# New load figures in a planner, and the order of loads and work that goes with them: retention and a gated layer on one core

## The chip, the cores and the metric

The kernel runs on 1 core of one Trainium2 chip. The metric is the device time of one execution in microseconds (us). The time before is 210.98 us, the median of 3 runs between 210.53 and 211.2 us. Below, PE is the engine that multiplies matrices (TensorE), DVE the vector engine, ACT the scalar engine, POOL the GpSimd engine, and SP the engine whose queue issues the loads.

## The reference

For each of 4 batches and 8 heads of 64 dimensions, a state of 64 x 64 decays at every one of 768 tokens and takes up the outer product of k and v; the token's output is q times that state. The 8 heads side by side are x (512 wide), and x goes through a gated layer.

```python
for t in range(S):
    state = gamma[None, :, None, None] * state + np.einsum('bhd,bhe->bhde', k[:, :, t], v[:, :, t])
    y[:, :, t] = scale * np.einsum('bhd,bhde->bhe', q[:, :, t], state)
...
for k in range(K):                      # K = 5 taps over the tokens
    gate_pre += conv_w[k][None, None, :] * xp[:, k:k + S, :]
gate = 1.0 / (1.0 + np.exp(-gate_pre))
val = x @ w_val
return (gate * val @ w_out).astype(np.float32)
```

## The kernel before, in words

The tokens are cut into 6 chunks of 128, so there are 24 pairs (chunk c, batch b), numbered g = 4c + b. One tile `att` of 1 MB holds for one g the transposed q and k, v by token, and k by token; four such tiles are in flight (`LB = 4`). A pair's retention is done in the chunked form: scores of q against k (into the PSUM tile `sy`), a mask on DVE (tile `u`), the product of the masked scores with v, the contribution of the state (`snap`, a copy of the PSUM tile `z_ps` made on ACT), and the update of the state in `z_ps`. Before a k or v is used for the state, POOL multiplies it by a decay table (`decay`, L355). The result y is multiplied on DVE by a table into x (`evac`, L519). Of x, ACT makes a rounded copy `xh` (L529), and POOL the rest `xl` (L534), so that a product in full precision is made from three products of rounded parts. The weights come as 64-bit numbers; each of the 8 weight tiles (`wst`, 0.5 MB) is converted by two operations on ACT (L559, L578), two on DVE (L563, L569), a sum on POOL (L582), then rounded on ACT (L592, `wvh` or `woh`), and POOL makes the rest (L596, `wvl` or `wol`). The five taps run on ACT (the first) and DVE (four, L610).

In the first chunk (g = 0 to 3) the state is empty. PE then has for each batch three blocks of 16 calls, all with small operands: the scores s (L379), the product y (L456, into the PSUM tile `ye`, of which there is one) and the two updates of the state z (L423). Later pairs are done in a visit v of 64 calls: the masked scores times v (L439), the state (L423), the state's contribution (L439), and the scores of the next pair (L366). The head h, scores (L366) and one half of a state update (L423) of g = 4, stands ahead of the first visit. The gated layer has 24 tiles V of 12 matmuls of 128 x 512 (`val`, L625) and 24 tiles O of 12 matmuls (`outp`, L659). V of chunk c and block m needs all four x of the chunk and the converted weight tile m: in order it takes `xh` with `wvh`, `xh` with `wvl`, `xl` with `wvh`. It writes one of two PSUM tiles `mm`, which comes free when DVE has multiplied the last one by the gate (`gated`, L640). The profile counts a call with 32-bit operands as two matmuls where they are small (a block of 16 calls is x32, a visit 128), and each matmul has a weight load of its own (PEld).

All of this is issued in an order that a planner in the program sets (`plan`, L79). Each step has an engine, a cost, what it reads and writes, and a due time. Due times come from two tables: LOADS (L704), the order of the first loads, and WORK (L707), a string in which p, s, y, z, h, v, V, O stand for the blocks above and w for a load and conversion of a weight tile. In LOADS, q is the q and k^T part of a batch of the first chunk (0.5 MB), v and k its v and k by token (0.25 MB each), a all but k (0.75 MB), t the small tables, w a weight tile. The planner then runs a model of the engines: whichever engine is free earliest takes, of the steps whose inputs are ready, the one with the lowest rank, and this gives the order in which the program lists the instructions. In the model a load lands `mb * PER_MB` after the load before it and not sooner than `FIRST_BYTE` after its issue (L246). Where the model sees PE wait ahead of the first V, it puts in filler matmuls on zeros (`filler`, L687, L689), whose results nothing uses. On the chip every engine then works off its own list in order, each instruction waiting for its inputs by semaphores.

SP issues all loads from one list, in order: a load waits until its buffer is free and until the load eight places ahead has landed. The tile of g = 4 goes into the buffer of g = 0 after its z, and so on.

Of the kernel before, what the change touches and what calls it, by code (L numbers as in the profile page):

```python
# [33 lines left out]
INTO, OUT_OF = 0.3, 0.134  # L34
COLD, WARM_AT = 1.85, 5.0
FIRST_PAGE, PAGE, FETCH, CROWDED = 94, 127.5, 3.0, 2.9
FIRST_BYTE, PER_MB = 4.1, 2.7
TABLES = (5.2, 9.3)

TIMES = {  # L40
# [222 lines left out]
def tile_retention_gated_mlp(  # L263
# [9 lines left out]
    nc = tc.nc  # L273
# [20 lines left out]
    small_sb = const.tile([P, small.shape[1]], F32, name="small_sb")  # L294
# [25 lines left out]
    def at(due, engine, cost, reads, writes, fn, *args):  # L320
        steps.append(Step(due, engine, cost, list(reads), list(writes), fn, args))
        return steps[-1]
# [371 lines left out]
    def first_sigmoid():  # L694
# [6 lines left out]


    CONV_LEAD, CHUNK = 7.0, 3.4
    LOADS = (("q", 0), ("t", 0), ("k", 0), ("v", 0), ("w", 0), ("a", 1), ("w", 1), ("a", 2), ("a", 3), ("k", 1), ("w", 2), ("k", 2), ("k", 3), ("w", 3))  # L704


    WORK = (  # L707
        "spysysszyyzzzVwwVwwhvVVOOvvOvOVvVvVVOvOvVVO"
        "vvVOvVvOVVOvOvVVOvvOVOvVOOvvvVVOVOOVVOVOOOO"
    )  # L710

    first_val = []
# [4 lines left out]
    def load_part_at(due, g, first, last):  # L717

        keys = [("att", g % LB, k) for k, part in (("qk", 0), ("vk", 2), ("kn", 3)) if first <= part < last]
        at(due, "DMA", 0.4, [], keys, load, g, slice(first, last)).mb = 0.25 * (last - first)  # L720
# [101 lines left out]
    def load_w_at(t, n):  # L822
        at(t, "DMA", 0.4, [], [wsts[n]], load_w, n).mb = 0.5
# [59 lines left out]
    at(0.2, "DVE", 0.25, [], [xbufs[0]] + [("x", 0, i) for i in range(B)], new_x, 0)  # L883
    for p, (kind, n) in enumerate(LOADS):
        t = 0.1 * p
        if kind == "t":
            at(t, "DMA", 0.4, [], ["small"], get, small_sb, small, nc.sync).mb = 0.2
        elif kind in "aqvk":
            load_part_at(t, n, *{"a": (0, 3), "q": (0, 2), "v": (2, 3), "k": (3, 4)}[kind])
        else:  # L890
            load_w_at(t, n)
    for x in range(2):
        for k, (engine, cost) in enumerate((("DVE", (0.42, 0.35)), ("ACT", (0.25, 0.2)))):
# [4 lines left out]
            )  # L898
    early = [n for kind, n in LOADS if kind == "w"]
    for n in ["cw"] + early:  # L900
        convert(5.5, n)

    t, whole = 6.0, {}
# [3 lines left out]
    for what in WORK:  # L907
# [7 lines left out]
        elif what == "s":  # L915
            t = max(t, 6.0 + CHUNK * i)
# [125 lines left out]
```

## Time and profile before

| | |
|---|---|
| runs | 210.98 us (210.53 to 211.2, 3 runs) |
| the profiled execution's own time | 210.8 us |
| its span | 209.0 us |
| PE busy | 199.7 us, 96% |
| DVE, ACT, POOL busy | 123.5, 110.2, 105.9 us |
| read from memory, written | 29.46 MB, 6.29 MB |

The span is the stretch from the first to the last recorded instruction; the execution's own time is 1.8 us longer. A line of the timeline gives the start in us, the duration in us, the engine, the line of the kernel, the operation, the tiles (written <- read), their shape and the count, and in brackets the idle time ahead of it and what ended it. Matmuls overlap: the start of the next line less the start of this one is what a line takes of PE's time.

### The profile page before, as it was taken

Reading aid. Unit: us, or ns where it says so; the run is one execution under the profiler, and the core shown is the slowest. Engines: PE = TensorE matmul, PEld = TensorE weight load, DVE = VectorE, ACT = ScalarE, POOL = GpSimd, SP = SyncE. Lnnn points to the kernel's source line nnn. Section 1 sums busy time; section 2 is a strip of 40 time slices with the busy share of each in tenths; the row PEclk is TensorE's granted clock in tenths of the full one; section 3 lists DMA queues with packets and bytes.
Section 4 is the critical chain, followed back from the end, with each engine's and each line's share of the span. In section 5 each row is a group of like instructions: output and inputs, shape, how many; then the busy total and the mean of one; then the engine's idle time right before and its main releaser. Section 6 shows DMA issues by size and latency. Waiting matters only on the chain.

```text
span 209.0 us, 7837 instructions
## 1 busy us (share of the span) xinstructions
PE 199.7 (96%) x3502; PEld 159.3 (76%) x3502; DVE 123.5 (59%) x189; ACT 110.2 (53%) x237; POOL 105.9 (51%) x93
## 2 busy tenths in 40 slices
PE   8967898999999999999999999999999999999994
PEld 3647676788888888788887888788787788878783
DVE  1586999952399814899129992227796259921100
ACT  3584687774667434685338654146364445413121
POOL 0189999999824582536627324526142353204200
PEclk9999999999999999999999999999999999999999
DMA  6999994557555508527275138348111100120122
GB/s 213 411 408 412 418 413 167 204 172 274 167 204 204 204 3 279 226 94 258 109 256 204 50 108 270 130 161 299 53 50 53 56 0 0 50 103 0 50 100 102
DMA packets 9253, 36.24 MB, mean 173 GB/s; under 512 B 1154, under 2 KB 1538, under 8 KB 6660
## 3 DMA queue, kind: packets, MB, share of 16 engines
q1 hardware_dynamic: 5472, 29.43, 37.7%
q10 hardware_dynamic: 3748, 6.32, 8.2%
q8 instruction: 27, 0.44, 0.9%
q14 instruction: 6, 0.05, 0.1%
HBM read 29.46 MB, written 6.29 MB: 171 GB/s over the span
## 4 chain that ended last, share of the span: by engine, by line
PE 89%; DMA 7%; issue 1%; DVE 1%; SPq 0%; ACT 0%; ACTq 0%
PE mm L659 33%; PE mm L625 33%; PE sy L439 11%; PE z_ps L423 5%; DMA att<-in_att_dram 5%; PE sy L366 5%; DMA cw_raw<-in_conv_w_dram 2%; PE sy L689 1%; PE sy L379 0%; DVE u L411 0%; PE ye L456 0%; DVE x L519 0%; SPq L342 0%; ACT gate L670 0%; SPq L545 0%
## 5 line engine op out<-in xcount | busy, mean ns | idle before, releaser
L610 DVE SCALAR_TENSOR_TENSOR acc<-x,cw_sb,acc 128x512 f32<-128x512 f32 x96 | 66.8, 750 | 2.7 <-ACT acc L608 2.1
L534 POOL TENSOR_TENSOR xl<-x,xh 128x512 fp32r<-128x512 f32 x24 | 30.9, 1288 | 44.0 <-ACT xh L529 44.0
L651 POOL TENSOR_TENSOR gvl<-gate,gvh 128x512 fp32r<-128x512 f32 x24 | 30.9, 1289 | 30.6 <-ACT gvh L647 30.6
L659 PE MATMUL mm<-woh,gvl 128*128 128x512 f32 (+1 forms) x100 | 38.7, 396 | 0.0
L659 PE MATMUL mm<-woh,gvh 128*128 128x512 f32 (+1 forms) x100 | 38.2, 390 | 0.0
L659 PE MATMUL mm<-wol,gvh 128*128 128x512 f32 (+1 forms) x100 | 37.9, 387 | 0.0
L625 PE MATMUL mm<-xl,wvh 128*128 128x512 f32 x96 | 34.4, 399 | 0.0
L625 PE MATMUL mm<-xh,wvh 128*128 128x512 f32 x96 | 32.0, 399 | 0.0
L355 POOL TENSOR_TENSOR att<-att,small_sb 128x512 f32<-128x512 f32 x24 | 25.1, 1049 | 12.4 <-DMA att<-in_att_dram 12.4
L640 DVE TENSOR_TENSOR gate<-mm,gate 128x512 f32<-128x512 f32 x24 | 16.5, 688 | 20.5 <-PE mm L625 18.1
L625 PE MATMUL mm<-xh,wvl 128*128 128x512 f32 x96 | 27.0, 397 | 0.0
L647 ACT CAST gvh<-gate 128x512 fp32r<-128x512 f32 x24 | 14.9, 619 | 22.1 <-DVE gate L640 22.0
L388 DVE TENSOR_TENSOR u<-sy,small_sb 128x512 f32<-128x512 f32 x20 | 13.7, 687 | 21.6 <-PE sy L366 21.6
L519 DVE TENSOR_TENSOR x<-sy,dec 128x512 f32<-128x512 f32 x20 | 13.7, 683 | 17.3 <-PE sy L366 12.5
L659 PEld LDWEIGHTS mm<-woh,gvl 128*128 128x128 f32 x100 | 18.7, 188 | 4.7 <-POOL gvl L651 0.5
L670 ACT COPY o_sb<-mm 128x512 f32<-128x512 f32 x23 | 13.5, 586 | 16.5 <-PE mm L659 16.1
L659 PEld LDWEIGHTS mm<-woh,gvh 128*128 128x128 f32 x100 | 18.7, 188 | 4.4 <-ACT o_sb L670 0.2
L617 ACT ACTIVATE gate<-acc 128x512 f32<-128x512 f32 x24 | 14.4, 600 | 14.1 <-DVE acc L610 7.8
L529 ACT CAST xh<-x 128x512 fp32r<-128x512 f32 x24 | 14.9, 619 | 13.0 <-DVE x L519 12.1
L659 PEld LDWEIGHTS mm<-wol,gvh 128*128 128x128 f32 x100 | 18.7, 188 | 3.8
L625 PEld LDWEIGHTS mm<-xl,wvh 128*128 128x128 f32 x96 | 18.0, 188 | 4.4
L625 PEld LDWEIGHTS mm<-xh,wvl 128*128 128x128 f32 x96 | 17.9, 188 | 4.3
(52 smaller groups left out, 248.2 us busy)
## 6 DMA issues: line engine op xcount, KB each, us to landing
att<-in_att_dram SPq DMA_DIRECT2D x20, 1024.0 KB, 5.3
out_dram<-o_sb ACTq DMA_DIRECT2D x23, 256.0 KB, 2.2
wst<-in_w_dram SPq DMA_DIRECT2D x8, 512.0 KB, 8.7
att<-in_att_dram SPq DMA_DIRECT2D x3, 768.0 KB, 7.2
att<-in_att_dram SPq DMA_DIRECT2D x5, 256.0 KB, 10.4
att<-in_att_dram SPq DMA_DIRECT2D x1, 512.0 KB, 3.6
out_dram<-gate ACTq DMA_DIRECT2D x2, 128.0 KB, 1.7
small_sb<-in_small_dram SPq DMA_DIRECT2D x1, 68.0 KB, 3.5
```

Source lines behind the costliest of these rows:

```text
L355: nc.gpsimd.tensor_tensor(v, v, vd_sb[:, c, :].unsqueeze(2).broadcast_to([P, 8, HALF]), op=ALU.mult)
L388: nc.vector.tensor_tensor(us[g], sy[:, :, 0:256].rearrange("p x (a t) -> p x a t", t=HALF), tri_sb.unsqueeze(1).unsqueeze(1).broadcast_to( ...
L439: nc.tensor.matmul(sy[cols, h, off:off + HALF], lhsT=lhsT, rhs=rhs, start=start, stop=True, skip_group_check=True,)
L529: nc.scalar.copy(xh[n][:, :, b], xs[n][:, :, b, HALO:])
L534: nc.gpsimd.tensor_tensor(xl[n][:, :, b], xs[n][:, :, b, HALO:], xh[n][:, :, b].bitcast(F32), op=ALU.subtract)
L610: nc.vector.scalar_tensor_tensor(acc, x[:, :, k:k + P], cw_sb[:, m, k:k + 1], acc, op0=ALU.mult, op1=ALU.add,)
L617: nc.scalar.activation(gate[n, m], accs.pop((n, m)), AF.Sigmoid)
L625: nc.tensor.matmul(vps[n, m], lhsT=w[:, m, ct * P:(ct + 1) * P], rhs=xx[n][:, ct].rearrange("p b t -> p (b t)"), start=(i == 0), stop=(i = ...
L640: nc.vector.tensor_tensor(gv, vps.pop((n, m)), gv, op=ALU.mult)
L647: nc.scalar.copy(gvs[n, m][0], gate[n, m])
L651: engine.tensor_tensor(gvl, gate.pop((n, m)), gvh.bitcast(F32), op=ALU.subtract)
L659: nc.tensor.matmul(ops[n, b, cs.start][:, 0:cs.stop - cs.start], lhsT=gg[:, b * P:(b + 1) * P], rhs=w[:, ct, cs], start=(i == 0), stop=(i ...
```

## The change

The planner's figures for loads are 3.0 us to the first byte and 2.65 us per MB instead of 4.1 and 2.7, the small tables count as 0.13 MB instead of 0.2, and the tables LOADS and WORK are others. No function, cost of an engine, tile or buffer is changed.

```diff
-FIRST_BYTE, PER_MB = 4.1, 2.7
+FIRST_BYTE, PER_MB = 3.0, 2.65
...
-    LOADS = (("q", 0), ("t", 0), ("k", 0), ("v", 0), ("w", 0), ("a", 1), ("w", 1), ("a", 2), ("a", 3), ("k", 1), ("w", 2), ("k", 2), ("k", 3), ("w", 3))
+    LOADS = (("q", 0), ("t", 0), ("v", 0), ("k", 0), ("a", 1), ("w", 0), ("w", 1), ("k", 1), ("k", 2), ("a", 2), ("k", 3), ("a", 3), ("w", 2), ("w", 3))
...
-        "spysysszyyzzzVwwVwwhvVVOOvvOvOVvVvVVOvOvVVO"
+        "spyszsyyzszyhVwzVwwVvwvVOvOvvOVOvvVVVvvOVvO"
...
-            at(t, "DMA", 0.4, [], ["small"], get, small_sb, small, nc.sync).mb = 0.2
+            at(t, "DMA", 0.4, [], ["small"], get, small_sb, small, nc.sync).mb = 0.13
```

The first place is PE's list around the first V. Before, with att_120, att_126 and att_129 the tiles of batches 1, 2 and 3 of the first chunk and att_206 that of g = 4, it reads:

```order
L423 MATMUL z_ps_94<-att_120 64x64 x16
L689 MATMUL sy_95<-const-float32-0.0 128x128 x4
L423 MATMUL z_ps_94<-att_126 64x64 x16
L625 MATMUL mm_428<-xh_217,wvh_89 128x512 x4
L423 MATMUL z_ps_94<-att_129 64x64 x16
L625 MATMUL mm_428<-xh_217,wvl_90 128x512 x4
L625 MATMUL mm_428<-xl_242,wvh_89 128x512 x4
L625 MATMUL mm_479<-xh_217,wvh_89 128x512 x4
L625 MATMUL mm_479<-xh_217,wvl_90 128x512 x4
L625 MATMUL mm_479<-xl_242,wvh_89 128x512 x4
L366 MATMUL sy_95<-att_206 64x64 x16
L423 MATMUL z_ps_94<-att_206 64x64 x8
```

Now, with att_128 and att_148 the tiles of batches 2 and 3 and att_218 that of g = 4, the same place reads:

```order
L423 MATMUL z_ps_94<-att_128 64x64 x16
L689 MATMUL sy_95<-const-float32-0.0 128x128 x4
L366 MATMUL sy_95<-att_218 64x64 x16
L423 MATMUL z_ps_94<-att_218 64x64 x8
L625 MATMUL mm_463<-xh_235,wvh_89 128x512 x4
L625 MATMUL mm_463<-xh_235,wvl_90 128x512 x4
L625 MATMUL mm_463<-xl_273,wvh_89 128x512 x3
L625 MATMUL mm_486<-xh_235,wvh_89 128x512
L625 MATMUL mm_463<-xl_273,wvh_89 128x512
L625 MATMUL mm_486<-xh_235,wvh_89 128x512
L423 MATMUL z_ps_94<-att_148 64x64 x16
```

The head of g = 4 has moved from behind the second V to ahead of the first; ahead of the first V stand the z of batches 0, 1 and 2 (the z of batch 1 earlier in the list), and that of batch 3 behind its fourteenth matmul, where before those of batches 2 and 3 stood around its first four.

The second place is POOL's list from its second instruction of the first chunk on, ending with the `xl` of batch 3. Before, it reads:

```order
L582 TENSOR_TENSOR cw_sb_87<-top_203,up_204 128x20
L534 TENSOR_TENSOR xl_242<-x_104,xh_217 128x4x128
L582 TENSOR_TENSOR top_209<-top_209,up_210 128x512
L582 TENSOR_TENSOR top_250<-top_250,up_251 128x512
L596 TENSOR_TENSOR wvl_90<-top_209,wvh_89 128x512
L534 TENSOR_TENSOR xl_242<-x_104,xh_217 128x4x128
L596 TENSOR_TENSOR wvl_90<-top_250,wvh_89 128x512
L355 TENSOR_TENSOR att_120<-att_120,small_sb_86 128x512
L534 TENSOR_TENSOR xl_242<-x_104,xh_217 128x4x128
L355 TENSOR_TENSOR att_126<-att_126,small_sb_86 128x512
L355 TENSOR_TENSOR att_129<-att_129,small_sb_86 128x512
L534 TENSOR_TENSOR xl_242<-x_104,xh_217 128x4x128
```

Now, with att_117 the tile of batch 1, it is one instruction longer; its first twelve rows are:

```order
L355 TENSOR_TENSOR att_117<-att_117,small_sb_86 128x512
L582 TENSOR_TENSOR cw_sb_87<-top_223,up_224 128x20
L582 TENSOR_TENSOR top_227<-top_227,up_228 128x512
L534 TENSOR_TENSOR xl_273<-x_104,xh_235 128x4x128
L596 TENSOR_TENSOR wvl_90<-top_227,wvh_89 128x512
L582 TENSOR_TENSOR top_268<-top_268,up_269 128x512
L534 TENSOR_TENSOR xl_273<-x_104,xh_235 128x4x128
L596 TENSOR_TENSOR wvl_90<-top_268,wvh_89 128x512
L355 TENSOR_TENSOR att_128<-att_128,small_sb_86 128x512
L534 TENSOR_TENSOR xl_273<-x_104,xh_235 128x4x128
L355 TENSOR_TENSOR att_218<-att_218,small_sb_86 128x512
L355 TENSOR_TENSOR att_148<-att_148,small_sb_86 128x512
```

The decay of batch 1 has moved to the front, and that of g = 4, which stood behind the first `xl` of batch 3, stands ahead of the decay of batch 3.

The third place is PE's list from the visit of g = 4 to that of g = 5. Now it reads:

```order
L439 MATMUL sy<-att,snap 64x64 x16
L366 MATMUL sy<-att 64x64 x16
L625 MATMUL mm<-xl,wvh 128x512 x4
L625 MATMUL mm<-xh,wvh 128x512 x4
L625 MATMUL mm<-xh,wvl 128x512
L439 MATMUL sy<-u,att 64x64 x16
```

Between the two visits stand 9 large matmuls; before there were 18. The numbers from visit to visit, from g = 4 on, are now 9, 11, 13, 11, 28, 7, 29, 7, 20, 24, 21, 7, 30, 38, 24, 12, 24, 57, 7, and before 18, 8, 21, 24, 12, 34, 8, 31, 12, 23, 12, 48, 12, 33, 7, 32, 30, 7, 7. After the last visit stand 177, before 173. In the list of loads on SP the first 14 follow LOADS; behind them stood g = 4, three weight tiles, g = 5 and 6, a weight tile, g = 7, and stand now g = 4, two weight tiles, g = 5, a weight tile, g = 6, a weight tile, g = 7.

More of the change, by code (lines that the diff above doesn't have):

```diff
@@ L703, in tile_retention_gated_mlp @@
     CONV_LEAD, CHUNK = 7.0, 3.4
-    LOADS = (("q", 0), ("t", 0), ("k", 0), ("v", 0), ("w", 0), ("a", 1), ("w", 1), ("a", 2), ("a", 3), ("k", 1), ("w", 2), ("k", 2), ("k", 3), ("w", 3))
+    LOADS = (("q", 0), ("t", 0), ("v", 0), ("k", 0), ("a", 1), ("w", 0), ("w", 1), ("k", 1), ("k", 2), ("a", 2), ("k", 3), ("a", 3), ("w", 2), ("w", 3))
     WORK = (
-        "spysysszyyzzzVwwVwwhvVVOOvvOvOVvVvVVOvOvVVO"
-        "vvVOvVvOVVOvOvVVOvvOVOvVOOvvvVVOVOOVVOVOOOO"
+        "spyszsyyzszyhVwzVwwVvwvVOvOvvOVOvvVVVvvOVvO"
+        "OvOVvvVVOvOVVvVOvVvVOvOVVOOvvVOVVOVVOOOOOOO"
     )
```

## Prediction

> **What bounds the kernel now.** I read the page first, then the stretches, then the timeline of PE, then landings. The page:
>
> ```profile
> PE 199.7 (96%) x3502; PEld 159.3 (76%) x3502; DVE 123.5 (59%) x189; ACT 110.2 (53%) x237; POOL 105.9 (51%) x93
> ...
> q8 instruction: 27, 0.44, 0.9%
> ...
> PE 89%; DMA 7%; issue 1%; DVE 1%; SPq 0%; ACT 0%; ACTq 0%
> ```
>
> The reader is to see that PE holds 89% of the chain that ended last. Cut at the first matmul of the first V and at PE's last, the stretches (PE's busy time stands first behind the length) say where it is not full:
>
> ```profile
> 0.00:23.39 23.39, 18.23 (x386) 12.39 (x387) 13.59 (x23) 14.69 (x32) 13.59 (x17) 1.00 0.94 366
> 23.39:205.99 182.60, 181.45 (x3122) 146.94 (x3116) 109.94 (x167) 95.09 (x205) 92.27 (x77) 1.00 0.41 150
> 205.99:209.02 3.03, 0.00 (x0) 0.00 (x0) 0.00 (x0) 0.37 (x1) 0.00 (x0) 1.00 0.25 87
> ```
>
> From 23.39 us on PE has work for all but 1.15 us, and the work is the same after the change: as many V, O and visits. The last copy and store behind PE (3.03 us) stay too. So there are two places for a gain or a loss: how much useful work PE has done when the dense part begins, and the few stalls in it. DMA is 94% busy in the first stretch. Now PE there, and around the head of g = 4:
>
> ```profile
> 15.75 1.00 PE L379 MATMUL sy<-att 64*64 64x128 f32 x32 [0.76 <-DMA att<-in_att_dram]
> 16.57 0.85 PE L456 MATMUL ye<-u,att 64*64 64x128 f32 x32
> ...
> 20.52 0.60 PE L689 MATMUL sy<-const-float32-0.0 128*128 128x128 f32 x3
> 22.12 0.71 PE L689 MATMUL sy<-const-float32-0.0 128*128 128x128 f32 x5 [1.00 <-issue]
> 22.77 0.69 PE L423 MATMUL z_ps<-att 64*64 64x64 f32 x32
> 23.39 1.20 PE L625 MATMUL mm<-xh,wvh 128*128 128x512 f32 x4
> ...
> 25.15 1.20 PE L625 MATMUL mm<-xh,wvl 128*128 128x512 f32 x4
> ...
> 27.12 1.10 PE L625 MATMUL mm<-xh,wvh 128*128 128x512 f32 x4
> 28.05 1.10 PE L625 MATMUL mm<-xh,wvl 128*128 128x512 f32 x4
> ...
> 30.01 0.69 PE L366 MATMUL sy<-att 64*64 64x64 f32 x32
> ...
> 30.87 1.20 PE L625 MATMUL mm<-xh,wvh 128*128 128x512 f32 x4
> ```
>
> A block of 32 takes 0.82 (s and y, 15.75 to 16.57) or 0.62 us (z, 22.77 to 23.39); a large matmul 0.233 (four from 27.12 to 28.05); a z between large matmuls takes 25.15 less 23.39 less four of them = 0.83; the head takes 0.86 (30.01 to 30.87).
>
> Two stalls are put down to "issue", to nothing that the program waits for. The second, and what follows it:
>
> ```profile
> 33.86 0.69 PE L439 MATMUL sy<-u,att 64*64 64x64 f32 x32
> ...
> 35.35 0.28 PE L366 MATMUL sy<-att 64*64 64x64 f32 x5
> 36.29 0.68 PE L366 MATMUL sy<-att 64*64 64x64 f32 x27 [0.66 <-issue]
> 36.90 0.50 PE L625 MATMUL mm<-xl,wvh 128*128 128x512 f32 x1
> ...
> 41.27 0.69 PE L439 MATMUL sy<-u,att 64*64 64x64 f32 x32
> ...
> 43.54 0.50 PE L659 MATMUL mm<-woh,gvh 128*128 128x512 f32 x1
> ...
> 52.80 0.69 PE L439 MATMUL sy<-u,att 64*64 64x64 f32 x32
> ...
> 54.86 0.50 PE L659 MATMUL mm<-woh,gvl 128*128 128x512 f32 x1
> ```
>
> Between the two stalls PE's rows count 254 matmuls (5 fillers, z 32, V 4, z 32, V 20, head 48, V 12, 101 of the visit). The queue q8, named instruction, brought 27 packets (0.44 MB) for 3502 matmuls with as many weight loads: one for about 130 matmuls. I read it so: PE's program comes in pages of about 127 matmuls, one page ahead. The stall at 22.12 ended a page asked for 127 matmuls earlier, which is 8 into the scores at 15.75, at about 15.95: a page took 6.2 us while loads filled the queues. Visits cost 2.06 us where nothing is late (52.80 to 54.86), but 3.04 (33.86 to 36.90) and 2.27 (41.27 to 43.54) here: 0.98 + 0.21 = 1.19 us lost.
>
> **The change part by part.** *Landings.* PE's wait for the a of batch 1, then the a of batch 2 and the tile of g = 4 (issue on SP, and from there to landing):
>
> ```profile
> 9.68 0.90 PE L379 MATMUL sy<-att 64*64 64x128 f32 x32 [0.21 <-DMA att<-in_att_dram]
> ```
>
> ```profile
> 4.91 0.43 SPq L342 DMA_DIRECT2D att<-in_att_dram  x1
> ```
>
> ```profile
> DMA to landing us min/median/max: 7.9/7.9/7.9
> ```
>
> ```profile
> 10.98 0.33 SPq L342 DMA_DIRECT2D att<-in_att_dram  x1
> ```
>
> ```profile
> DMA to landing us min/median/max: 11.7/11.7/11.7
> ```
>
> So what ended at 2.32 MB of the list landed at 9.65, at 3.57 MB at 12.8, at 4.32 MB (the a of batch 3, PE's wait at 15.75) at 15.6, and g = 4 at 22.7. Between these by proportion, k of batch 1 now ends at 3.07 MB, 11.6 us; a of batch 2 at 4.07 MB, 14.7 (before 12.8). The a of batch 3 ends at 5.07 MB, by the same 2.7 us per MB at 17.6 (before 15.6); g = 4 keeps its place. The big loads that PE needs come 2 us later. POOL hides most of it, since it was the later one already:
>
> ```profile
> 10.56 0.22 POOL L582 TENSOR_TENSOR cw_sb<-top,up 128x20 int32<-128x20 int32 x1 [3.98 <-DVE top L569]
> ...
> 18.70 1.05 POOL L355 TENSOR_TENSOR att<-att,small_sb 128x512 f32<-128x512 f32 x1
> 19.70 1.28 POOL L534 TENSOR_TENSOR xl<-x,xh 128x512 fp32r<-128x512 f32 x1
> 20.93 2.05 POOL L355 TENSOR_TENSOR att<-att,small_sb 128x512 f32<-128x512 f32 x2
> ```
>
> From y (PE, 16.57) to the multiply on DVE and to `xh` on ACT:
>
> ```profile
> 17.69 0.68 DVE L519 TENSOR_TENSOR x<-ye,base 128x512 f32<-128x512 f32 x1
> ```
>
> ```profile
> 18.41 0.62 ACT L529 CAST xh<-x 128x512 fp32r<-128x512 f32 x1 [0.16 <-DVE x L519]
> ```
>
> *POOL's train.* A decay costs 1.0 (18.70 to 19.70), a sum, `xl` or `wvl` 1.23 (19.70 to 20.93). Now the decay of batch 1 comes first: 11.6 to 12.6, then the small sum to 12.8, and four of 1.23 to 17.7. The next, `xl` of batch 1, needs its x. The scores of batch 2, at 14.7, stand ahead of y of batch 1 on PE, so y starts at 15.5, the multiply 1.12 and `xh` another 0.72 later, and `xl` 0.62 after that at 18.0. With `wvl` POOL is at 20.4, the decay of batch 2 is done at 21.4, `xl` at 22.7, and the decay of g = 4, landed by then, at 23.7.
>
> *PE up to the first V.* z of batch 2 could start at 21.45. But a page ends three matmuls into it: up to the boundary before, PE's list has 212 matmuls and 9 of y of batch 1, so that one falls at 15.75, and by the 6.2 us the page comes at 21.95. z ends at 22.55. Eight fillers follow, which cost 0.60 and 0.65 before (20.52 to 21.12, 22.12 to 22.77): 23.8. The head takes 0.86; its state part comes after 23.7 anyway. The first V starts at 24.65, later than 23.39, but with the head behind it. Compared where the first two V, all z and the head are done: before 30.87, now 24.65 + 24 x 0.233 + 0.83 = 31.07. The head stage loses 0.2 us. Bounds: a gain of 0.4 (the page after 5.7 us, as the one whose wait ended at 36.29 took from its boundary 32 into the head, about 30.55) and a loss of 0.9 (a of batch 2 only at 15.4, near the 15.6 of the next load before).
>
> *DVE.* The third V writes the bank that the first gate multiply frees. Seven taps, a mask and two taps now stand ahead of it:
>
> ```profile
> 22.77 4.31 DVE L610 SCALAR_TENSOR_TENSOR acc<-x,cw_sb,acc 128x512 f32<-128x512 f32 x6
> 27.39 0.69 DVE L640 TENSOR_TENSOR gate<-mm,gate 128x512 f32<-128x512 f32 x1 [0.30 <-PE mm L625]
> ```
>
> A tap costs 0.72; a mask I take as the multiply, 0.69. x of batch 3 and two weight steps are done at about 22.8 (y of batch 2 after the multiply of batch 1, scores and mask of batch 3, y at 19.85, and four DVE operations), so the multiply ends at 22.8 + 9 x 0.72 + 2 x 0.69 = 30.65. PE reaches its matmul at 24.65 + 14 x 0.233 + 0.83 + 7 x 0.233 = 30.4. A stall of 0.2; bounds 0 and 0.9 (one tap more).
>
> *Visits.* The page boundary in the visit of g = 4 falls 106 matmuls into it, at 34.8; the page was asked for in the z of batch 3, at 28.6, and comes after 5.7 to 6.2 us. So the 1.19 us of before go, and I set 0.1 in their place. Late next is the following page: asked for at 34.8, needed 97 matmuls into the visit of g = 5, behind 22 of this visit (0.6 with its way out), 9 large matmuls (2.1), and 97 at 1.5: at 39.0, 4.2 us later. That is the first rival.
>
> *At nothing.* The filler ahead of the first scores is gone; PE waits for loads all the same. The closer visits need masks, decays and x in time: 8 matmuls lay between the visits that began at 41.27 and next, and the stretch has 1.15 us of idle time in all; DVE has its mask and multiply (1.4 us) inside 9 x 0.233 = 2.1 us. Without that cover a close visit would lose up to 0.7.
>
> *The sum.* 0.2 + 0.2 + 0.1 - 1.19 = -0.69 us: the profiled 210.8 would become 210.1; from the median of 210.98, **210.3 us**.
>
> **The rivals.** *First, slower: the page behind a load.* The load of g = 8 goes out when the visit of g = 4 has read its q. In the trace of before that issue, and the page asked for at 36.29, found in the DMA rows for 39.8 to 40.8 us:
>
> ```profile
> 35.62 0.33 SPq L342 DMA_DIRECT2D att<-in_att_dram  x1
> ```
>
> ```profile
> q8 instruction: 1, 0.02, 7.3%
> ```
>
> Asked for 0.67 us after the load, the page came 3.8 us later, when 1 MB had passed. If that repeats, it takes 6.2 us where 4.2 are there, and the visit of g = 5 stalls 2.0: 210.3 + 2.0 - 0.1 = 212.2. It turns on whether PE passes the boundary ahead of the load: by count it lies 10 matmuls (0.15 us) behind the last that reads q, and the issue came 0.27 us after that (35.35 to 35.62), so PE is 0.1 us early; a stall of half a us there would put it behind. Chance 0.17. The Trainium skill (DMA: Bandwidth & Descriptors, Queues, rings and completion order) says that each DMA engine takes turns between queues, packet by packet; by that rule the page would wait for one packet only, and this rival would cost nothing. The page at 40 us speaks against the rule.
>
> *Second, no gain: the train slips.* POOL waits for x of batch 1 and g = 4 with no slack. With the bound of 0.9 in place of 0.2: 211.0. For it: the loads are 2 us later; against: PE stands behind the page by 0.5 us of its own. Chance 0.2.
>
> *Third, a larger gain.* The page comes sooner and DVE in time: -0.4 - 1.19 + 0.1 = -1.5 at best; with part of either, 209.8. Chance 0.13.
>
> *Fourth, the stalls are no pages.* The Trainium skill (Runtime: NRT & Kernel Launch, Instruction fetch mechanics) says that programs are fetched in blocks ahead of use, and that a crossing is mostly hidden. Two stalls of 1.00 and 0.66 us at 254 matmuls' distance disagree. Were the 1.19 us the crowded stretch's own, they would stay: 210.98 + 0.2 + 0.2 = 211.4. Chance 0.05.
>
> **How the numbers follow.** The forecast has 0.45, with a range of its own of 209.8 to 210.9. About 0.3%, 0.63 us, is what a measurement of this kernel can tell from no change: the limits are 210.35 and 211.6. The forecast lies on the first: 0.27 faster, 0.17 same, 0.01 slower. The second rival gives 0.15 same, 0.05 slower; the third 0.12 faster, 0.01 same; the first 0.17 slower; the fourth 0.04 same, 0.01 slower. Faster 0.39, same 0.37, slower 0.24. The range runs from 209.5 (third) to 212.1, which leaves out half of the first rival.
>
> **What would show it.** Right: the first V at 24.4 to 24.9 with the head ahead of it, visits of g = 4 and 5 of about 2.1 us, PE idle under 0.5 us from there to its end. Wrong: a row with "issue" at about 39 in the visit of g = 5 (first rival); the first V after 25.2, behind POOL or x (second); stalls on "issue" that do not fit pages (fourth).

## The result, and the profile after

The changed kernel takes 212.91 us, the median of 22 runs between 210.87 and 215.5, against 210.99 (210.53 to 213.46, 22 runs) for the kernel before: slower by 0.3% to 0.8% (ratio 1.0057, 95% interval 1.0034 to 1.0081). That ratio leaves out runs more than 1.5% above a kernel's best, which is why it is smaller than the medians' 1.009. The forecast was 210.3, faster.

What strikes first is not the median but the spread: 4.6 us, where before has 0.8 with one run outside. Each timed run comes with its span and its mean granted clock, and by these the 22 runs fall into three groups: five at full clock with spans of 209.1 to 209.5 (before at full clock: a mean of 209.2), six at full clock with 210.5 to 211.8, and eleven with a clock of 0.984 to 0.992 and spans up to 213.7. Of the 1.92 us between the two medians, about 1.3 are there in the full-clock runs alone (their median is 212.27); the rest comes with the lower clock. The study below is on what makes the groups. The profile shown here is of the second one; its own time is 212.6, its span 210.8. The page:

```profile
PE 200.9 (95%) x3502; PEld 159.7 (76%) x3502; DVE 123.4 (59%) x189; ACT 109.3 (52%) x237; POOL 106.0 (50%) x93
...
q8 instruction: 27, 0.44, 0.8%
...
PE 79%; DMA 3%; POOL 3%; issue 1%; DVE 1%; ACT 1%; POOLq 0%; ACTq 0%
```

The same work, but PE holds 79% of the chain that ended last instead of 89%; POOL has joined it. The stretches, cut at the first matmul of the first V and at PE's last:

```profile
0.00:25.23 25.23, 19.89 (x435) 13.55 (x435) 13.85 (x23) 15.16 (x34) 14.00 (x17) 1.00 0.95 368
25.23:207.80 182.57, 181.01 (x3068) 146.13 (x3068) 109.54 (x167) 93.72 (x203) 91.98 (x77) 1.00 0.40 146
```

The dense part is as long as before (182.57 against 182.60), though the head of g = 4 has been taken out of it and the stretch ahead has become 1.84 longer. PE there, in the timeline:

```profile
13.02 0.69 PE L423 MATMUL z_ps<-att 64*64 64x64 f32 x32 [1.49 <-POOL att L355]
...
15.38 0.90 PE L379 MATMUL sy<-att 64*64 64x128 f32 x32 [1.04 <-DMA att<-in_att_dram]
16.07 0.88 PE L456 MATMUL ye<-u,att 64*64 64x128 f32 x32
17.94 0.90 PE L456 MATMUL ye<-u,att 64*64 64x128 f32 x32 [1.00 <-DVE x L519]
...
22.19 0.69 PE L423 MATMUL z_ps<-att 64*64 64x64 f32 x32
...
25.23 1.20 PE L625 MATMUL mm<-xh,wvh 128*128 128x512 f32 x4 [0.35 <-ACT xh L529]
...
30.83 0.39 PE L625 MATMUL mm<-xl,wvh 128*128 128x512 f32 x1
31.31 0.47 PE L625 MATMUL mm<-xh,wvh 128*128 128x512 f32 x1
```

Three waits stand in the 7 us from 11.5 to 18.5: for the decay of batch 1, for the a of batch 2, and for x. The y of batch 1 runs at 16.07 (before: 11.99), because the scores of batch 2, which wait for their load, stand ahead of it; the first V starts at 25.23, waiting for the last `xh`. The third V waits about 0.25 us for its bank at 31.31 (0.48 from the row ahead, less one matmul of 0.233). Now the visits of g = 4 and 5:

```profile
34.04 0.69 PE L439 MATMUL sy<-u,att 64*64 64x64 f32 x32
...
35.53 0.92 PE L366 MATMUL sy<-att 64*64 64x64 f32 x32
36.38 1.20 PE L625 MATMUL mm<-xl,wvh 128*128 128x512 f32 x4
...
38.68 0.69 PE L439 MATMUL sy<-u,att 64*64 64x64 f32 x32
...
41.14 0.27 PE L439 MATMUL sy<-att,snap 64*64 64x64 f32 x1 [0.80 <-issue]
...
41.80 0.97 PE L625 MATMUL mm<-xh,wvl 128*128 128x512 f32 x3
```

The visit of g = 5 takes 3.12 us (38.68 to 41.80) and stalls in its 96th matmul for nothing that the program names; that of g = 4 takes 2.34, its last block 0.92 instead of 0.65, so a shorter stall of about 0.26 is hidden in that row. SP issued the load of g = 8 here:

```profile
35.77 0.33 SPq L342 DMA_DIRECT2D att<-in_att_dram  x1
```

The boundary of the page, 106 matmuls into the visit of g = 4, was passed at about 35.9, behind that issue, and the packet of q8 started at 38.8, three us later. This is the first rival's picture.

### The profile page after: what moved, and what is told of

Read it like the earlier page. It is cut to its first block, busy times and chain, and to the rows that moved or that the text cites. A ratio compares the mean times of both kernels' runs of the same rounds, so it can differ in the third digit from the quotient of the medians.

```text
span 210.8 us, 7837 instructions
## 1 busy us (share of the span) xinstructions
PE 200.9 (95%) x3502; PEld 159.7 (76%) x3502; DVE 123.4 (59%) x189; ACT 109.3 (52%) x237; POOL 106.0 (50%) x93
## 4 chain that ended last, share of the span: by engine, by line
PE 79%; DMA 3%; POOL 3%; issue 1%; DVE 1%; ACT 1%; POOLq 0%; ACTq 0%
PE mm L625 32%; PE mm L659 29%; PE sy L439 10%; PE sy L366 4%; PE z_ps L423 4%; DMA att<-in_att_dram 3%; DVE top L569 1%; POOL top L582 1%; POOL xl L534 1%; POOL att L355 0%; POOL wol L596 0%; POOL gvl L651 0%; ACT acc L608 0%; DVE acc L563 0%; ACT xh L529 0%
## 5 line engine op out<-in xcount | busy, mean ns | idle before, releaser
L651 POOL TENSOR_TENSOR gvl<-gate,gvh 128x512 fp32r<-128x512 f32 x24 | 30.9, 1289 | 34.2 <-ACT gvh L647 34.2
L534 POOL TENSOR_TENSOR xl<-x,xh 128x512 fp32r<-128x512 f32 x24 | 30.9, 1289 | 26.0 <-ACT xh L529 26.0
L659 PE MATMUL mm<-woh,gvl 128*128 128x512 f32 (+1 forms) x100 | 37.8, 391 | 0.0
L659 PE MATMUL mm<-woh,gvh 128*128 128x512 f32 (+1 forms) x100 | 37.6, 389 | 0.0
L625 PE MATMUL mm<-xl,wvh 128*128 128x512 f32 x96 | 35.6, 403 | 0.1
L625 PE MATMUL mm<-xh,wvh 128*128 128x512 f32 x96 | 34.5, 403 | 0.4 <-ACT xh L529 0.3
L388 DVE TENSOR_TENSOR u<-sy,small_sb 128x512 f32<-128x512 f32 x20 | 13.8, 689 | 35.9 <-PE sy L366 26.7
L625 PE MATMUL mm<-xh,wvl 128*128 128x512 f32 x96 | 26.5, 396 | 0.0
L625 PEld LDWEIGHTS mm<-xh,wvh 128*128 128x128 f32 x96 | 17.8, 188 | 5.5 <-ACT xh L529 0.8
L617 ACT ACTIVATE gate<-acc 128x512 f32<-128x512 f32 x24 | 14.4, 600 | 12.2 <-POOL gvl L651 6.3
L529 ACT CAST xh<-x 128x512 fp32r<-128x512 f32 x24 | 14.7, 617 | 8.6 <-DVE x L519 8.5
```

What stands on the lines that cost most here:

```text
L388: nc.vector.tensor_tensor(us[g], sy[:, :, 0:256].rearrange("p x (a t) -> p x a t", t=HALF), tri_sb.unsqueeze(1).unsqueeze(1).broadcast_to( ...
L529: nc.scalar.copy(xh[n][:, :, b], xs[n][:, :, b, HALO:])
L534: nc.gpsimd.tensor_tensor(xl[n][:, :, b], xs[n][:, :, b, HALO:], xh[n][:, :, b].bitcast(F32), op=ALU.subtract)
L617: nc.scalar.activation(gate[n, m], accs.pop((n, m)), AF.Sigmoid)
L625: nc.tensor.matmul(vps[n, m], lhsT=w[:, m, ct * P:(ct + 1) * P], rhs=xx[n][:, ct].rearrange("p b t -> p (b t)"), start=(i == 0), stop=(i = ...
L651: engine.tensor_tensor(gvl, gate.pop((n, m)), gvh.bitcast(F32), op=ALU.subtract)
```

## The experiments

Three theories ran through them. A: pages of PE's program come behind loads (the first rival). B: the head of the kernel is later, because loads, x and the decays are (the second rival's ground). C: waits of PE in the head drop its granted clock, which was in no part of the forecast.

**e1: the changed kernel, page boundaries 30 matmuls earlier.** Each of the ten first matmuls is cut into four.

```
-            ye[:, i % 2], lhsT=..., rhs=warm.broadcast_to([P, 512]),
+        for k in range(4):
+            ye[:, i % 2, k * P:(k + 1) * P], lhsT=..., rhs=warm.broadcast_to([P, P]),
```

> The changed kernel, with each of the ten warm-up matmuls of 512 columns cut into four of 128: the same time on PE and the same order of everything else, but 30 more matmuls ahead, so that every page boundary falls 30 matmuls earlier. In the visit of g = 4 it moves from 106 matmuls in (behind the release of the load of g = 8) to 76 (ahead of it). Theory A (the loss is pages that come behind a load, at visits too close together to wait for them): the stall of 0.8 us in the visit of g = 5 goes, the median falls by 0.8 us or more to 212 or below, and the spread of 4.6 us between runs shrinks to below 2. Theory B (the loss is the head of the program: later loads, POOL's and ACT's trains): the median stays within 0.4 us of 212.9 and the spread stays.

212.27 us (211.97 to 213.77, 6 runs; ratio 1.0083, 1.0051 to 1.0114). The visits of g = 4 and 5 took 2.06 and 2.07 us: moving the boundary took both stalls away. But PE's waits have a new row, in y of batch 3:

```profile
PE ye L456 <- issue: 0.7, 1, 0.7
```

So A's mechanism holds, but this shift puts another boundary in the way, and the first V came at 25.93. The spread fell below 2 us, as A had it; the median stayed 0.3 above its 212.

**e2: the same shift in the kernel before.**

> The kernel before with the same cut of the warm-up matmuls, page boundaries 30 matmuls earlier, nothing else. Both theories: the stall of 0.66 us in the visit of g = 4 is a page asked for in the crowd; it is asked for about 0.5 us earlier and needed 0.4 us earlier, so the time stays within 0.4 us of 210.98 and the spread stays below 1 us. It is the control for the cut itself: if the cut costs something by its own, it shows here.

211.01 us (ratio 1.0003, 0.9979 to 1.0027). The stall in the visit of g = 4 went; in the timeline of PE a wait for the gate multiply took its place:

```profile
39.00 0.47 PE L659 MATMUL mm<-woh,gvh 128*128 128x512 f32 x1 [0.94 <-DVE gate L640]
```

In the order of before, a page stall covers a wait for DVE that comes next; taking it away gains nothing that can be measured. The expected spread of under 1 us was missed: it is 3.2 (210.25 to 213.46), with three of the 12 runs at a clock of 0.976 to 0.991.

**e3 and e4: the new figures with one new table each**, the loads (e3) or the work (e4), the other table as before.

```
e3:  FIRST_BYTE, PER_MB = 3.0, 2.65;  new LOADS, old WORK
e4:  FIRST_BYTE, PER_MB = 3.0, 2.65;  old LOADS, new WORK
```

> The new figures and the new order of loads, with the old string of work. Visits of g = 4 and 5 stand 19 large matmuls apart, nearly as before (18). Theory A: no wide spread (below 1.5 us), and a time of 211 to 211.8 (only the loss in the head, which the later loads give). Theory B: the loads of batches 2 and 3 land 2 us later as in the changed kernel, so 212 to 213 with the wide spread.

> The new figures and the new string of work, with the old order of loads. Visits of g = 4 and 5 stand 7 large matmuls apart, closer than in the changed kernel. Theory A: a wide spread of 3 us or more and a median of 212.5 or more, with a stall on issue in one of the visits of g = 4 to 8. Theory B: the loads are on time again, 211.3 or below and a narrow spread.

213.04 us (ratio 1.0108, 1.0064 to 1.0152, 6 runs) and 214.42 (1.018, 1.014 to 1.022). The new work alone is slower than the whole, and the new loads alone can't be told from it (213.04 against 212.91, and the intervals overlap), so neither half can be called the part that costs. The loads came out about as B expected (212 to 213 with a wide spread), with a wait of 1.8 us on "issue" in its profile's fillers. The work came out at A's time, but without the stall on "issue" in a visit that A expected: the largest waits of its profile are two for loads ahead of scores, 3.3 us together. The page's row of the granted clock is the new thing to see; of e4:

```profile
PEclk9985999996999999999999999999999999999999
```

Twice PE ran at half its clock for a while, from 14.8 to 21.6 us and from 48.9 to 52.3.

**e5: as e1, each filler on ye issued twice**, to fill the waits of the head.

```
-        for dst in ((ye[:, 0, 256:512],) if ring == "ye" else ...
+        for dst in ((ye[:, 0, 256:512],) * 2 if ring == "ye" else ...
```

> The changed kernel with the cut warm-up matmuls of the first experiment, and each of its five fillers on ye issued twice, in the gaps of the head (10 to 15 and around 19.7 us); the sy fillers and the order of all else as they were. Two of six runs of the first experiment took 213.7 us, the others 212.0 to 212.5. Theory C (in some runs PE is idle for so much of one 3.4 us window that its granted clock falls to a half for a window or more): no run over 212.9, the others stay at 212 to 212.5. Theory B (spread from loads and trains): about one run in three still over 213.

214.72 us (ratio 1.0154, 1.0102 to 1.0207): a miss. The planner's other fillers were where they had been, and the profiled run waited ahead of the z of batch 0, whose k now lands behind v:

```profile
8.60 1.13 PE L423 MATMUL z_ps<-att 64*64 64x64 f32 x32 [1.86 <-POOL att L355]
```

Behind it the block takes 0.91 instead of 0.62, and the clock stood at half from 7.8 to 14.6 us. That is not all: two other runs have spans of 213.5 and 214.5 at a clock of 1.0 and 0.997, and no profile shows why.

**e6: the kernel before, its fillers 16 columns wide** instead of 256 and 128; same count, same order, same pages, so that only PE's useless work is less.

```
-        for dst in ((ye[:, 0, 256:512],) if ring == "ye" else (sy[:, 0, 384:512],) * 2):
+        for dst in ((ye[:, 0, 256:272],) if ring == "ye" else (sy[:, 0, 384:400],) * 2):
```

> The kernel before with its fillers as many as they were, but of 16 columns instead of 256 or 128, so that PE is idle for about 4 us more of the first 23. The order, the page boundaries and the loads stay. Theory C: the granted clock falls to 0.5 in the head in most runs, and a good part of the runs lies at 212.5 or above, as in the changed kernel. Theory B: the fillers hold up nothing and their work is not used, so 210.8 to 211.1 and a spread below 1 us.

214.77 us (ratio 1.0146, 1.01 to 1.0192); all six runs had a mean clock of 0.960 to 0.984. Two stretches of its profile, with the granted clock behind the five engines' busy times:

```profile
13.05:19.88 6.83, 5.37 (x118) 4.76 (x110) 3.65 (x6) 3.23 (x6) 6.35 (x6) 0.50 1.03 408
23.29:30.12 6.83, 6.83 (x77) 5.32 (x77) 5.36 (x8) 3.70 (x8) 5.83 (x6) 0.50 1.01 395
```

In the second PE is busy without a gap, all of it at half clock. C stands: work that nobody uses was holding the clock, and without it the kernel loses 3.8 us of median. It did not hold it always: of 34 runs of the kernel before timed beside e13 to e16, six had a clock of 0.976 to 0.992 (a 35th took 275 us at 0.659, which nothing here explains).

**e7 and e8: one more figure.** e7 is the changed kernel with 2.85 us per MB, which fits the landings better; e8 the kernel before with the figures 3.0, 2.85 and 0.13 and its own two tables.

> The changed kernel with 2.85 us per MB in the planner instead of 2.65: the figure by which the loads behind the first MB land as the trace of before has them (the a of batch 2 at 14.8, g = 4 at 23.3). LOADS and WORK as in the changed kernel; the planner now places six fillers ahead of the scores of batch 2 and z of batch 1 behind y of batch 1. If the figures' error on the later loads makes the loss (theories B and C), a median of 211 to 211.8 and a spread below 1.5 us. If the strings make it (theory A: visits of g = 4, 5 and 6 now 12 and 16 apart), 212 or above.

> The kernel before, its LOADS and WORK, with 3.0 us to the first byte, 2.85 us per MB and 0.13 MB for the tables: figures fitted to the trace. Fillers move behind y of batch 3. Theories B and C: 210.6 to 211.2 with a narrow spread, since the order is nearly that of before and the fillers stand in the gaps. Should the fitted figures help by themselves, 210.4 or below.

214.48 us (ratio 1.0144, 1.0103 to 1.0186) and 213.62 (1.0129, 1.0082 to 1.0175): both missed. e8 is the plainer: with the tables of before and full clock in its profile, the other figures alone cost about 2 us of span (211.1 and 211.6 at full clock), in waits that before has not, the largest of them in the O tiles:

```profile
PE mm L659 <- POOL wol L596: 1.3, 2, 1.2
```

Figures and tables only work together: other figures make another order of everything, and it is no better for being made with them.

**e9: the changed kernel once more.**

> The changed kernel once more, nothing edited, for a second profile and more times. Of the 22 runs so far, 11 had a mean granted clock of 0.998 or more, with spans of 209.1 to 211.8 us, and the others 0.998 to 0.984, with spans up to 213.7; before had 209.2 in the middle. Theory B (the head stage loses 1.1 us by later loads) says that no run is much below 210.2, so a second profile shows the first V at 25.0 or later and the same waits. Theory C (the clock) says that the times spread again over 210.9 to 215.5, with a mean of about 212.5, and that those above 213 have a clock of 0.992 or less. Theory A (the page behind the load of g = 8) says that the visit of g = 5 takes about 3.1 us in the profile again, or that it takes 2.1 and the run is about 1 us shorter.

213.45 us (4 runs, spans of 211.2 and 211.7 at full clock, 211.6 and 211.9 at 0.984). C had kept times above 213 for lower clocks; the profiled run has 213.45 at full clock. The second profile of the same program, PE in the visits of g = 4 and 5, and the load of g = 8:

```profile
35.35 0.30 PE L366 MATMUL sy<-att 64*64 64x64 f32 x8
35.89 0.58 PE L366 MATMUL sy<-att 64*64 64x64 f32 x24 [0.24 <-issue]
...
42.24 0.27 PE L439 MATMUL sy<-att,snap 64*64 64x64 f32 x1 [1.89 <-issue]
```

```profile
35.59 0.33 SPq L342 DMA_DIRECT2D att<-in_att_dram  x1
```

The stall at the boundary in the visit of g = 4 (0.24) shows in the row itself. It leaves PE 0.3 us behind the load of g = 8, and the next page takes 6.3 us (35.89 to 42.24) and stalls the visit of g = 5 by 1.89. In the first profile the lateness was 0.1 and the stall 0.80. The first V came at 25.06, as B had it.

**e10: the changed kernel, its fillers on ye 512 columns wide** instead of 256 (five calls, ten rows); count, order, loads and pages unchanged.

```
-        for dst in ((ye[:, 0, 256:512],) if ring == "ye" else ...
+        for dst in ((ye[:, 0],) if ring == "ye" else ...
```

> The changed kernel; the ten fillers on ye (rows L689 of 128x256) are 512 columns wide instead of 256, so that each keeps PE busy twice as long (0.52 instead of 0.26 us); their number, the order, the loads and the page boundaries are as they were. The wait for the decay of batch 1 (1.49 us) then shrinks to nothing and that for the scores of batch 2 (1.04) to about 0.5, so that PE idles at most 1.7 us in any 3.4 us of the head, where the changed kernel has 2.07 (11.96 to 15.37). Theory C: no run loses its clock there; the spread shrinks to about 1.5 us and the median falls to 211.5 to 212. Theories A and B: nothing useful is done earlier, so the median stays at 212.5 to 213 and the spread is as wide.

213.34 us over nine runs, one of them 1089 us, which nothing here explains and which is left out below. At full clock the spans are 209.1, 209.5 and then 210.7 to 212.2, the two groups again; two runs of eight had a clock of 0.992. The profile fell in the first group, and there the same two visits and the same load read:

```profile
34.01 0.69 PE L439 MATMUL sy<-u,att 64*64 64x64 f32 x32
...
35.50 0.65 PE L366 MATMUL sy<-att 64*64 64x64 f32 x32
36.08 1.20 PE L625 MATMUL mm<-xl,wvh 128*128 128x512 f32 x4
...
38.37 0.69 PE L439 MATMUL sy<-u,att 64*64 64x64 f32 x32
...
40.43 0.96 PE L625 MATMUL mm<-xh,wvl 128*128 128x512 f32 x3
```

```profile
35.74 0.33 SPq L342 DMA_DIRECT2D att<-in_att_dram  x1
```

```profile
q8 instruction: 1, 0.02, 5.8%
```

PE passes the boundary, 10 matmuls into the block at 35.50, at about 35.6, now 0.1 us ahead of the load; the page's packet lies in the DMA rows of 36 to 37 us instead of at 38.8, and the visit of g = 5 takes 2.06. The span is 209.5, with the first V at 25.20 as late as ever. So in the profiles the two groups differ by who is first at 35.7 us, and a run of the first group still stands 0.5 above the kernel before. The expected median was missed, since I had put the groups down to the clock.

In these profiles, what decides who is first lies one page earlier. That page is asked for 28 matmuls into the z of batch 3, just ahead of the load of g = 7. The z and that load, first in the changed kernel's own profile, then in e10:

```profile
28.70 0.69 PE L423 MATMUL z_ps<-att 64*64 64x64 f32 x32
```

```profile
29.50 0.33 SPq L342 DMA_DIRECT2D att<-in_att_dram  x1
```

```profile
28.67 0.69 PE L423 MATMUL z_ps<-att 64*64 64x64 f32 x32
```

```profile
29.48 0.33 SPq L342 DMA_DIRECT2D att<-in_att_dram  x1
```

By count the request comes at 29.16 and 29.13, each about 0.35 us ahead of the load, and in e9, e11 and e12 the lead is the same. Yet the page's packet started at 33.6 in the changed kernel and at 31.0 in e10. From 29.2 us on, 1.67 MB had been moved by 33.5 in the first, and 0.63 MB by 30.9 in the second: the difference is about the 1 MB load. Where the packet came late (4.4 to 4.8 us behind the request, in the changed kernel, e9, e11 and e12), PE stalled at the boundary by 0.24 to 0.5 us and so passed it behind the load of g = 8; in e10 it came after 1.9 us and PE did not stall. What lets the page ahead in one run and not in another, at the same lead, no run shows.

**e11 and e12: y of batch 1 earlier**, ahead of z of batch 1 on PE and with its multiply in DVE's idle time at 12.2; e12 has the wide fillers as well.

```
+        for s in (named(first_y, 1), named(evac, 1)):
+            order.remove(s)
+            order.insert(order.index(named(first_state, 1)), s)
```

> The changed kernel; on PE, y of batch 1 stands ahead of z of batch 1 and the scores of batch 2, instead of behind them, and on DVE its multiply into x stands where DVE waits now (12.2 to 13.2), instead of behind the mask of batch 2. All else is in the same order. Theory B (the scores of batch 2, which wait for a load till 15.4, hold up y of batch 1, x and the rounded parts behind it): y of batch 1 runs at 11.5 instead of 16.07, y of batch 2 starts at about 17.3 instead of 17.94, the first V at about 24.6 instead of 25.2, and a run at full clock gains 0.6 to 0.7 us. Theory C: the idle of PE ahead of z of batch 1 shrinks by 0.8 us too, so the spread also shrinks. Theory A: nothing changes from the first V on.

> Both edits, of the fillers and of y of batch 1. The three fillers ahead (rows count six) take 3.1 us instead of 1.6, so y of batch 1 starts at about 13.1, its multiply waits for it till 13.9, and z of batch 1 at 13.9. Theories B and C together: the best of the four, 211 to 211.5 with a spread under 1.5 us, and the first V at 24.6 to 24.8; theory A: the visit of g = 5 still stalls by 0.8 to 1.0 where the page comes behind the load, which keeps it above the kernel before.

212.46 us (12 runs, one of 1077 left out below; ratio 1.0047, 1.0019 to 1.0075) and 212.9 (11 runs; 1.0062, 1.0031 to 1.0093). The 211 to 211.5 expected of e12 was missed, as was the spread under 1.5 us: the medians are still a mix of groups, and e12 has 208.7, 209.2, 209.5, 209.8 and 211.1, 211.3, 211.6, 211.6 at full clock. The mechanism came as expected; PE in e12:

```profile
12.47 0.90 PE L456 MATMUL ye<-u,att 64*64 64x128 f32 x32
...
17.22 0.90 PE L456 MATMUL ye<-u,att 64*64 64x128 f32 x32 [1.08 <-DVE u L411]
...
24.51 1.20 PE L625 MATMUL mm<-xh,wvh 128*128 128x512 f32 x4
```

The y of batch 2 starts at 17.22 instead of 17.92 (e10), and the first V at 24.51 instead of 25.20. The profile of e11 fell in a run that was twice at half its clock, with the first V at 26.12.

**e13 to e16: the page boundaries moved, the head left alone.** The two fillers ahead of the head of g = 4 (8 rows) become 20 small calls (40 rows), which puts every boundary behind them 32 matmuls earlier and leaves those ahead where they were. Both pages above are moved by it: the one by the load of g = 7 as well as the one by the load of g = 8. e14 adds the wide fillers, e16 the earlier y, e15 both.

```
+    def short_filler(ring):
+        for k in range(10):
+            x, rows, cols = ((0, LO, LO), (1, LO, HI), (0, HI, HI), (1, HI, LO))[k % 4]
+            nc.tensor.matmul(sy[cols, x, 384:448], lhsT=zero[rows]..., rhs=zero[rows]..., ...)
...
+        for step in order[order.index(named(first_state, 2)):order.index(named(head, 4))]:
+            if step.fn is filler:
+                step.fn = short_filler
```

> The changed kernel; the two fillers ahead of the head of g = 4 (8 rows of 128x128, 1.09 us) are 20 calls on 64 x 64 each (40 rows, about 0.8 us), so that every page boundary behind them lies 32 matmuls earlier, and nothing ahead of them changes. The boundary in z of batch 3 (0.34 us ahead of the issue of the load of g = 7) then falls about 0.5 us earlier, and that in the visit of g = 4 (0.12 us behind or 0.11 us ahead of the issue of the load of g = 8) at its 74th matmul, 0.5 us earlier. Theory A, the race of page and load: the visits of g = 4 and 5 take 2.06 to 2.12 us, and the runs at full clock are all of the first group, spans of 209.1 to 209.7, median under 211.5 if the clock holds. Theory C: the clock still drops in a quarter to a half of the runs, by the idle time of 2.0 us at 12 to 15 us. Theory B: no run is below the 209.1 that the changed kernel has at its best.

> The same, and the ten fillers on ye 512 columns wide, so that PE idles at most 1.7 us in any 3.4 us of the head. Theories A and C together: neither stall nor lower clock, nearly all runs within spans of 209.1 to 209.8, median 211.0 to 211.4. If the clock still drops as often as in e13, the idle time in the head is not what drops it.

> The same as e14, and y of batch 1 on PE and its multiply on DVE ahead of z of batch 1. Theory B: the first V at about 24.4 instead of 25.2, and 0.5 to 0.7 us less than e14: spans of 208.5 to 209.1, median 210.3 to 210.7, as fast as the kernel before or faster by up to 0.3%. If B is wrong and what counts is only from the first V on, as e14.

> As e13 with y of batch 1 and its multiply earlier, and the fillers on ye as wide as in the changed kernel. Theory B: 0.5 to 0.7 us less than e13 at full clock, spans of 208.5 to 209.1. Theory C: the wait ahead of z of batch 1 is half filled by y now, but a profile of this order (y earlier, narrow fillers) showed 1.95 us of idle time between 14.8 and 18.2 us and a lower clock there, so the clock drops in a third to a half of the runs, and the median is above that of e15.

| 12 runs each | median us | ratio, 95% | runs at full clock: spans | lower clock |
|---|---|---|---|---|
| e13 pages | 211.61 | 1.0041 (1.0012 to 1.0069) | 7: 209.2 to 210.0, mean 209.56 | 5 |
| e14 pages, wide | 211.57 | 1.0023 (1.0004 to 1.0043) | 11: 209.3 to 210.3, mean 209.80 | 1 |
| e16 pages, y | 211.67 | 1.0014 (0.9989 to 1.004) | 6: 208.5 to 210.1, mean 209.13 | 6 |
| e15 pages, y, wide | 211.11 | 1.0005 (0.9974 to 1.0036) | 9: 208.7 to 209.6, mean 209.21 | 3 |

The expected medians were missed by 0.1 to 0.4 us in e13, e14 and e15. In the profile of e13 a page wait of 0.58 us was left, in the first V. Its visits of g = 4 and 5, and its load of g = 8, which the boundary (74 matmuls into the visit of g = 4, at about 35.4) now precedes by 0.6 us:

```profile
34.25 0.69 PE L439 MATMUL sy<-u,att 64*64 64x64 f32 x32
...
36.32 1.20 PE L625 MATMUL mm<-xl,wvh 128*128 128x512 f32 x4
...
38.61 0.69 PE L439 MATMUL sy<-u,att 64*64 64x64 f32 x32
...
40.67 0.72 PE L625 MATMUL mm<-xh,wvl 128*128 128x512 f32 x2
```

```profile
35.98 0.33 SPq L342 DMA_DIRECT2D att<-in_att_dram  x1
```

A: with the boundaries where the change has them (the changed kernel, e9 to e12), 17 of 31 full-clock runs had spans above 210.4; with them moved, none of 33. e9 to e12 and e13 to e16 ran on different chips, and the changed kernel was not timed again beside e13 to e16; the kernel before, timed beside each set, had medians of 210.8 to 211.05 throughout, and e1, with moved boundaries on a third chip, has full-clock spans of 210.2 and 210.3. C: with narrow fillers in the head 31 of 61 runs had a clock under 0.995 (the changed kernel, e9, e11, e13, e16), with wide ones 9 of 43 (e10, e12, e14, e15), about the share of the kernel before (6 of 34). B: the earlier y is worth 0.43 us (e13 to e16) and 0.59 (e14 to e15) at full clock. What a lower clock costs, in e16's profile:

```profile
15.06:21.89 6.83, 5.01 (x98) 4.52 (x98) 2.20 (x3) 3.23 (x7) 6.72 (x7) 0.50 1.02 412
```

PE is busy for 5.01 of these 6.83 us, in the middle of the head's longest chain; its first V came at 26.99, the span was 211.4. The price differs from run to run: in e14 the one low run has a span of 210.0, and its row of the clock shows where it fell:

```profile
PEclk9799999999999999999999999999999999999999
```

There it came at 7.5 us and cost 0.2 against the mean. The place alone does not set the price: in e15's profile a like drop at 8.7 us stands in a run of 210.9, 1.7 above the mean. No version beats the kernel before: the best, e15, is level with it.

## Why the prediction was wrong, point by point

**The head stage (0.2 us, bounds -0.4 and +0.9): mis-sized, it took the upper bound.** The a of batch 2 was to land at 14.7 and let PE start at 15.38, near the bound of 15.4. I had drawn the landings between two loads of before by proportion, across an order of loads that was about to change. Everything behind followed as worked out: y, x, `xh`, POOL, and the first V at 25.23 instead of 24.65. The 24 matmuls of the first two V, all z and the head were done at about 32.0 (31.31 and three matmuls), 1.1 us later than before, where 0.2 and the gate's 0.2 were forecast. e12 shows the link: with y out from behind the waiting scores the first V comes 0.7 us earlier.

**The gate wait (0.2): right**, 0.25.

**The 1.19 us of page stalls that go: right in a part of the runs.** In e10 both visits take 2.07 and 2.06 us, as forecast, and the span of 209.5 stands 0.5 above that of before: the head's 1.1 less 1.2, and some 0.5 behind the visit of g = 5, in no wait of more than 0.3 us, whose cause stays open. Such runs last 210.87 to 211.2, the second rival's 211.0. e2 adds a warning that I hadn't drawn: in the order of before the same stall could be removed for no gain.

**The 0.1 in their place, and the first rival's chance of 0.17: this step failed.** The rival's price was 2.0 us on the visit of g = 5, and its condition that PE pass the boundary behind the issue of the load of g = 8. The condition was right: by count PE was 0.1 to 0.6 us late in four profiles (changed kernel, e9, e11, e12), with stalls of 0.80, 1.89, 1.07 and 1.34, all under that price, and 0.1 ahead in e10, with none. But I took 0.1 us ahead as the forecast. By my own numbers the page before it was asked for at 28.6 and due 5.7 to 6.2 us later, 34.3 to 34.8, and needed at 34.8: no slack at all. It took 6.7, 6.9, 6.8 and 7.2 us in the same four profiles, having been asked for only 0.35 us ahead of the load of g = 7, so that the one late page made the next one late. I had weighed the load of g = 8 against the next page, and never the load of g = 7 against this one; the term of 5.7 to 6.2 us is where the prediction first failed. A margin of 0.1 us against a spread of half a us is a coin; 17 of 31 full-clock runs fell on the other side. e13 to e16 had none, but they give this page a lead of 1.8 to 1.9 us as well as the next one a lead of 0.6, so they do not tell which of the two counts. The second group's mean span is 211.1, against 209.3 for the first.

The Trainium skill (DMA: Bandwidth & Descriptors, Queues, rings and completion order), with its turns between queues packet by packet, would have the page wait for one packet of the load. The traces speak against that: asked for 0.1 to 0.6 us behind the load of g = 8, the page's packet started three to four us later, and in e10, asked for ahead, within the next us.

**The clock: in no rival at all.** I had taken the granted clock of 1.00 in every stretch of before as a property of the kernel. It was largely one of its order: e6 shows that before holds it, in most runs, by its fillers. The planner puts fillers where its model sees PE wait; with loads that it believes earlier than they are, it saw less waiting than there was (PE still waited 1.04 us behind the filler ahead of the scores of batch 2). Half of the changed kernel's runs, 13 of 26, lost their clock once or more.

**The fourth rival, that the stalls are no pages, fell**: three shifts by count alone (e1, e2, e13) moved or removed them.

## What to carry to other kernels

When two requests of a forecast lie within a few tenths of a microsecond of each other, forecast both outcomes with about even chances. Look at every such pair, and at the earliest first, since a late one there decides the next; then look at the distribution of times and the granted clock of each run before explaining a median. A wait is also a matter of clock: ask of each new wait of PE what keeps PE busy meanwhile, and whether that filler is sized by the same model that misjudged the wait. And a more exact figure in a planner is no gain in itself; the order found with it has to be timed as a whole.

## What the runs showed of the hardware

A lower clock came in records of 3.41 or 6.83 us at 0.50 of full speed, behind waits that were each under 2 us. In the 3.41 us ahead of such a record PE was idle for 1.4 to 2.0 us in e3, e4, e16, the first of e6 and the second of e11, but only for 0.7 to 1.0 at the start of e5, e7, e11, e14 and e15, and ahead of the second of e6. The Trainium skill (TensorE: Matmul & The Clock Gate, Part 1: The HAM clock gate) gives the halving and a free-running window of about 3.4 us, which these records fit, and asks for an idle window of that length, which none of these profiles had. What drops the clock is open: the changed kernel's own profile had 2.09 us idle from 11.96 to 15.37 and kept its clock, and the kernel before kept it with 1.74 from 15.00 to 18.41. Only the counts of runs tell the fillers apart (31 of 61 against 9 of 43).

A page of PE's program (about 127 matmuls with their weight loads) took 5.3 to 7.2 us from being asked for to being used in the eight cases of four profiles (changed kernel, e9, e11, e12) in which its packet came late, with a 1 MB load issued within 0.6 us of the request. The packet started 3.0 to 4.8 us after the request there, and the matmul that waited ran 2.2 to 2.4 us after the packet. In e10 the packets of the same two pages started 1.9 and 0.8 us after their requests.
